# Sliding-window attention and a sentence-level MoE on one core: a fixed-order pipeline in place of a scheduled one

## Chip, cores, metric

The kernel runs on one core of one Trainium2 chip. The metric is the device time of one execution, in microseconds. Each run is marked fast or slow by its state. A ratio compares the fast runs alone of a kernel with fast runs of the kernel before, taken in the same rounds and on the same chip; the interval beside it is the 95% interval. A time in us is the median of all runs, slow ones included, so a ratio is not quite the ratio of two medians; where a slow run moves a median, the text says so. By these ratios a kernel counts as faster or slower if the difference is clear of 2%.

TensorE does the matrix products (matmuls) and writes them to PSUM, its accumulator memory; VectorE and ScalarE do the elementwise work, GpSimd some of the rest; the DMA engines move data between main memory (HBM) and SBUF, the working memory of the engines. MoE stands for mixture of experts, here the dense layers after attention.

## The reference

```python
B, H, S, D = 8, 8, 576, 64                       # attention
scores = q @ k.T / sqrt(D), allowed where |i - j| <= 32
attn   = softmax(scores);  a = attn @ v
x = a, heads side by side                        # (8, 576, 512)

pooled = x.mean(axis=1)                          # MoE: one expert per batch
logits = pooled @ w_gate                         # 8 experts
e      = argmax(logits);  g = softmax(logits)[e]
out    = g * (relu(x @ w1[e]) @ w2[e])           # 512 -> 1024 -> 512
```

The expert of a batch is known only when its whole attention is done. Its weights are 4.2 MB in fp32.

## The kernel before

A scheduler orders the instructions; the source says only what depends on what. The parts that matter here:

```python
def attention(b):
    # q, k, v: five loads each, 128 positions x 8 heads x 64: rows of 256 bytes
    ...
    nc.vector.tensor_copy(dst[:, 0:4, :, :], srt[:, 0:4, :, :])        # cast to bf16
    ...
    for hp in range(4):                                                # q and k: 40 transposes
        tp = ps1.tile([P, S], BF16, name="tp", tag="psA")
        for t in range(NST):
            nc.tensor.transpose(tp[:, SO[t] : SO[t] + ST[t]],
                src[0 : ST[t], t, 2 * hp : 2 * hp + 2, :], id_bf[0 : ST[t], 0 : ST[t]])
        nc.vector.tensor_copy(dst[:, hp, :], tp)                       # step 1 on both sides
    ...
    nc.tensor.matmul(sp[h][:, 0:mw], id_bf, ma, start=True, stop=False)   # -400 mask, by matmul
    nc.tensor.matmul(sp[h][0:J, off : off + RL[kb]], kTs[...], qTs[...], start=False, ...)
    nc.scalar.activation(et[h][:, eo : eo + mw], sp[h][:, 0:mw], Exp, scale=0.125)
    ...
    for t in range(NST):                                               # attention times V
        contribs = [(t, SO[t] - RLO[t], stl, 0)]                       # own keys: 128 columns
        if t >= 1:       contribs.append((t - 1, SO[t] - RLO[t - 1], 32, 0))
        if t + 1 < NST:  contribs.append((t + 1, 0, 32, stl - 32))
        for ci, (kb, lo, m, pr) in enumerate(contribs):                # shape outside,
            for h in range(H):                                         # heads inside
                nc.tensor.matmul(avp[pr : pr + m, base : base + 65],
                    Es[h][0:J, EOFF[kb] + lo : EOFF[kb] + lo + m], vaug[0:J, kb, h, :],
                    start=(ci == 0 and (h % 4) == 0), stop=False, tile_position=(0, pr))
        # reciprocal of the row sums and product on VectorE, four transposes, copy on ScalarE
    ...
def moe(xTt, lgi, gwb, b):
    nc.sync.dma_start(w1s32, moe_w1[ds(ereg, 1)][0]...)                # fp32
    nc.vector.tensor_copy(w1s, w1s32)                                  # cast on VectorE
    ...
for b in range(B):
    xTt = attention(b)
    if prev is not None: moe(*prev)
    lgi, gwb = gate(xTt)
    prev = (xTt, lgi, gwb, b)
```

The softmax here doesn't subtract the row's maximum and nothing guards it: scores larger than these inputs give would overflow.

## Time and profile before

| | before |
|---|---|
| median of its four runs in the first comparison | 386.8 us (383.93 to 389.44; the fourth took 1344.75 and is an outlier) |
| one middle batch | 42.3 us |
| TensorE busy, share of the span | 80% |
| mean granted TensorE clock | 0.852 |
| 16 DMA engines busy on loads and stores | 70.6% |

A group's row in the profile has line, engine, operation, output <- inputs, shapes and count; then busy time and the mean duration of one in ns; then the idle time ahead of it and what ended that. Matmul durations overlap, so what one matmul costs is read from a run of them. The chain of waits has start, length and what ran; `x16` is sixteen instructions merged. From the groups of the kernel before, attention times V:

```profile
L221 PE MATMUL avp<-vaug,etile 128*32 128x65 f16 (+3 forms) x832 | 44.9, 212 | 0.0
```

### The profile page before, as it was taken

The numbers are of one execution on the slowest core, as the hardware profiler recorded it, in microseconds if no ns is written. First come the engines' busy times: TensorE is split into PE (matmuls) and PEld (weight loads), VectorE is DVE, ScalarE is ACT, GpSimd is POOL, SyncE is SP. The second block draws the span as 40 slices with busy tenths as digits, with TensorE's granted clock in tenths as the row PEclk, the third lists the DMA queues.
The fourth block names the chain that finished last, engine by engine and source line by source line (L and its number), as shares of the span: only waits on it lengthen the run. The fifth ranks groups of instructions, "written<-read, shape, count | busy, mean of one in ns | idle before, by whom it ended". The sixth has DMA issues, their size and how long they took to land.

```text
span 384.9 us, 6511 instructions
## 1 busy us (share of the span) xinstructions
PE 307.4 (80%) x2656; PEld 176.6 (46%) x2656; DVE 165.9 (43%) x349; ACT 153.8 (40%) x353; POOL 7.9 (2%) x31
## 2 busy tenths in 40 slices
PE   0397498699958997699969997799859995893395
PEld 0234244474445554475345554565337444551262
DVE  0634562651467153652476055633385046501310
ACT  1044126163622536153723455253716362352052
POOL 1400000000000000000000000000000000000000
PEclk9998558589995999599986997599978999598599
DMA  9999049905889189936897289927996495015803
GB/s 160 210 208 162 3 157 346 202 7 160 278 273 212 51 219 381 222 67 179 305 285 161 83 236 371 195 48 211 345 258 119 149 292 218 0 54 181 325 0 124
DMA packets 130861, 71.74 MB, mean 186 GB/s; under 512 B 113936, under 2 KB 113936, under 8 KB 130832
## 3 DMA queue, kind: packets, MB, share of 16 engines
q1 hardware_dynamic: 130832, 71.33, 70.6%
q8 instruction: 21, 0.34, 0.4%
q14 instruction: 8, 0.07, 0.1%
HBM read 61.88 MB, written 9.44 MB: 185 GB/s over the span
## 4 chain that ended last, share of the span: by engine, by line
PE 70%; DVE 17%; DMA 6%; issue 4%; POOL 1%; SPq 0%; ACT 0%; DVEq 0%; POOLq 0%; ACTq 0%
PE op L340 18%; PE hpa L322 11%; PE hpb L326 10%; PE tp L162 8%; PE spAB L185 7%; PE avp L221 6%; PE spAB L194 6%; DVE xs L235 5%; DMA w2s<-in_moe_w_dram 4%; DVE w1s L312 4%; DVE w2s L314 4%; PE xtp L245 4%; DMA w1s<-in_moe_w_dram 2%; DVE linv L232 2%; DVE kbf L148 1%
## 5 line engine op out<-in xcount | busy, mean ns | idle before, releaser
L322 PE MATMUL hpa<-xTt,w1s 128*128 128x288 f16 x256 | 77.3, 331 | 12.2 <-DVE w1s L312 12.2
L326 PE MATMUL hpb<-xTt,w1s 128*128 128x288 f16 x256 | 76.6, 328 | 0.0
L203 ACT ACTIVATE etile<-spAB 128x480 f16<-128x480 f32 (+1 forms) x128 | 54.7, 550 | 48.3 <-PE spAB L194 47.4
L340 PE MATMUL op<-w2s,hT 128*128 128x512 f16 (+1 forms) x320 | 71.3, 380 | 0.0
L245 PE MATMUL xtp<-id_f,xs 128*128 128x128 f16 (+1 forms) x160 | 25.1, 254 | 41.0 <-DVE xs L235 40.2
L250 ACT COPY xTt<-xtp 128x512 f16<-128x512 f16 (+1 forms) x40 | 21.7, 542 | 83.2 <-PE xtp L245 83.2
L340 PEld LDWEIGHTS <-hT 128*128 128x128 f16 (+1 forms) x320 | 31.4, 100 | 37.2 <-issue 3.4
L347 ACT ACTIVATE osb<-op,gwb 128x512 f32<-128x512 f32 (+1 forms) x40 | 27.4, 686 | 43.7 <-PE op L340 43.7
L221 PE MATMUL avp<-vaug,etile 128*32 128x65 f16 (+3 forms) x832 | 44.9, 212 | 0.0
L330 ACT ACTIVATE hT<-hpa 128x288 f16<-128x288 f32 x64 | 26.2, 410 | 42.7 <-PE hpa L322 42.7
L221 PEld LDWEIGHTS <-etile 128*32 128x32 f16 (+3 forms) x832 | 37.1, 110 | 5.8 <-issue 1.6
L322 PEld LDWEIGHTS <-w1s 128*128 128x128 f16 x256 | 28.6, 112 | 23.0 <-DVE w1s L312 12.3
L266 DVE COPY lg<-lgp 1x8 f32<-1x8 f32 x8 | 1.2, 154 | 86.3 <-PE lgp L261 86.2
L232 DVE RECIPROCAL linv<-avp 128x8 f32<-128x8 f32 (+1 forms) x40 | 8.1, 203 | 67.1 <-PE avp L221 67.1
L245 PEld LDWEIGHTS <-xs 128*128 128x128 f16 (+1 forms) x160 | 9.8, 104 | 55.8 <-DVE xs L235 52.6
L326 PEld LDWEIGHTS <-w1s 128*128 128x128 f16 x256 | 28.5, 111 | 10.5
L235 DVE TENSOR_TENSOR xs<-avp,linv 128x256 f16<-128x256 f32 (+1 forms) x80 | 30.1, 417 | 1.4
L194 PE MATMUL spAB<-qTs,kTs 64*128 64x192 bf16 (+2 forms) x320 | 29.0, 249 | 0.0
L162 PE MATMUL tp<-id_bf,qbf 128*128 128x128 bf16 (+1 forms) x160 | 17.3, 236 | 14.3 <-DVE qbf L148 12.8
L333 ACT ACTIVATE hT<-hpb 128x288 f16<-128x288 f32 x64 | 25.9, 405 | 0.0
L255 DVE TENSOR_REDUCE pooledT<-xTt 128x4 f32<-128x2304 f16 x8 | 20.4, 2553 | 11.3 <-ACT xTt L250 11.3
L194 PEld LDWEIGHTS <-kTs 64*128 64x128 bf16 (+1 forms) x320 | 11.4, 97 | 29.8 <-issue 27.0
(51 smaller groups left out, 220.3 us busy)
## 6 DMA issues: line engine op xcount, KB each, us to landing
w1s<-in_moe_w_dram SPq DMA_DIRECT2D x8, 2048.0 KB, 8.1
w2s<-in_moe_w_dram SPq DMA_DIRECT2D x8, 2048.0 KB, 13.3
raw_q<-in_q_dram SPq DMA_DIRECT2D x32, 256.0 KB, 7.3
raw_k<-in_k_dram SPq DMA_DIRECT2D x32, 256.0 KB, 5.2
raw_v<-in_v_dram SPq DMA_DIRECT2D x32, 256.0 KB, 3.6
out_dram<-osb SPq DMA_DIRECT2D x32, 256.0 KB, 2.2
raw_q<-in_q_dram SPq DMA_DIRECT2D x8, 128.0 KB, 5.1
raw_k<-in_k_dram SPq DMA_DIRECT2D x8, 128.0 KB, 4.9
```

Of the source, the lines that this page charges most:

```text
L162: nc.tensor.transpose(tp[:, SO[t] : SO[t] + ST[t]], src[0 : ST[t], t, 2 * hp : 2 * hp + 2, :], id_bf[0 : ST[t], 0 : ST[t]],)
L185: nc.tensor.matmul(sp[h][:, 0:mw], id_bf, ma, start=True, stop=False, skip_group_check=True,)
L194: nc.tensor.matmul(sp[h][0:J, off : off + RL[kb]], kTs[hoff : hoff + D, hp, KO[kb] : KO[kb] + J], qTs[hoff : hoff + D, hp, RLO[kb] : RHI[kb]],
L203: nc.scalar.activation(et[h][:, eo : eo + mw], sp[h][:, 0:mw], mybir.ActivationFunctionType.Exp, bias=0.0, scale=0.125,)
L221: nc.tensor.matmul(avp[pr : pr + m, base : base + 65], Es[h][0:J, EOFF[kb] + lo : EOFF[kb] + lo + m], vaug[0:J, kb, h, :], start=(ci == 0 ...
L235: nc.vector.tensor_tensor(xs[0:stl, bk * 256 : (bk + 1) * 256].rearrange("p (h4 d) -> p h4 d", h4=4), hv[:, bk, :, 0:64], linv[0:stl, bk, ...
L245: nc.tensor.transpose(xtp[:, dt, 0:stl], xs[0:stl, dt * P : (dt + 1) * P], id_f16[0:stl, 0:stl],)
L322: nc.tensor.matmul(hpa, lhs, xTt[:, dt, 0:N1A], start=(dt == 0), stop=(dt == NDT - 1),)
L326: nc.tensor.matmul(hpb, lhs, xTt[:, dt, N1A:S], start=(dt == 0), stop=(dt == NDT - 1),)
L330: nc.scalar.activation(hT[:, ft, 0:N1A], hpa, mybir.ActivationFunctionType.Relu)
L340: nc.tensor.matmul(op[0:stl, :], hT[:, ft, SO[t] : SO[t] + stl], w2s[:, ft, :], start=(ft == 0), stop=(ft == NFT - 1),)
L347: nc.scalar.activation(osb[0:stl, :], op[0:stl, :], mybir.ActivationFunctionType.Copy, bias=0.0, scale=gwb[0:stl],)
```

## The change

The intent: take the order out of the scheduler's hands, hide attention's VectorE and ScalarE work under the dense MoE matmuls of the batch two before, load q and k in rows of 2304 bytes, cast weights in the DMA, and replace the mask matmuls by one product after the exponential. Positions come in interleaved (nine to a row of the load), so q and k are transposed in 64-row pieces and un-interleaved by a strided copy. Attention works on two heads per tile, with even and odd heads cut differently because V is loaded flat. The MoE runs in pieces of four matmuls between the pieces of attention. The core of the diff, shortened:

```diff
+    ctx.enter_context(tc.manual_schedule())
...
+            for name, dst in (("q", qT), ("k", kT)):
+                xb = castp.tile([P, J, 2, D], BF16, name=f"{name}bf", tag="qkbf", bufs=4)
+                nc.vector.tensor_copy(xb, r.rearrange("p h j d -> p j h d"))
+                for j in range(J):
+                    for pp in range(2):
+                        nc.tensor.transpose(tps[pp][:, j, :], xb[lo : lo + G, j, :, :], ...)
+                for pp in range(2):
+                    nc.vector.tensor_copy(t, tps[pp].rearrange("p j g -> p g j"))
+                yield
...
-                    nc.tensor.matmul(
-                        sp[h][:, 0:mw], id_bf, ma,
+            nc.vector.tensor_tensor(et, et, mask, ALU.mult)
...
+        nc.gpsimd.tensor_copy(vaug[:, :, 0:D], vraw)
...
-            for ci, (kb, lo, m, pr) in enumerate(contribs):
-                for h in range(H):
+            for h in (0, 2, 4, 6, 1, 3, 5, 7):
+                ...   # two parts per head: 128 columns, then 64 columns
+                for t, off, m, pr in parts:
                     nc.tensor.matmul(
...
-        nc.vector.tensor_copy(w1s, w1s32)
+        nc.gpsimd.dma_start(w1s, moe_w1[ds(ereg, 1)][0]...)     # fp32 -> fp16 in the DMA
...
+                # last MoE tile (64 rows): two column halves, tile_position=(0, 64 * c)
...
+    for n in range(B + LEAD):                                   # LEAD = 2
+        gens = [moe(n - LEAD), attention(n)]                    # one piece of each in turn
+        run_all(gens)
```

## The prediction

> **What bounds the kernel now.** I read the page first, then the chain of waits by time, then a table of stretches of one middle batch, then the timeline of that batch engine by engine.
>
> ```profile
> span 384.9 us, 6511 instructions
> ...
> PE 307.4 (80%) x2656; PEld 176.6 (46%) x2656; DVE 165.9 (43%) x349; ACT 153.8 (40%) x353; POOL 7.9 (2%) x31
> ...
> PEclk9998558589995999599986997599978999598599
> ...
> PE 70%; DVE 17%; DMA 6%; issue 4%; POOL 1%; SPq 0%; ACT 0%; DVEq 0%; POOLq 0%; ACTq 0%
> ...
> L167 DVE COPY qTs<-tp 128x576 bf16<-128x576 bf16 x32 | 14.2, 443 | 2.1 <-PE tp L162 1.0
> ```
>
> The chain that ended last is TensorE for 70% and VectorE for 17%; no other engine is near full. The clock row has a dip in each of the later batches: part of TensorE's "busy" is half-speed work.
>
> One batch (180.42 to 223.3 us), by stages; the columns are stretch, length, then each engine's busy time, granted clock, DMA share, GB/s:
>
> ```profile
> 180.42:184.30 3.88, 3.88 (x43) 2.59 (x42) 3.65 (x17) 0.89 (x3) 0.26 (x1) 1.00 0.87 203
> 184.30:190.50 6.20, 6.20 (x57) 2.16 (x56) 1.97 (x4) 5.56 (x14) 0.00 (x0) 1.00 0.86 321
> 190.50:202.20 11.70, 6.97 (x122) 4.99 (x120) 8.12 (x15) 3.55 (x7) 0.00 (x0) 0.87 1.08 294
> 202.20:214.30 12.10, 11.44 (x69) 7.78 (x70) 6.54 (x10) 5.44 (x16) 0.00 (x0) 0.71 0.61 128
> 214.30:223.30 9.00, 9.00 (x49) 4.02 (x48) 0.00 (x0) 3.54 (x7) 0.00 (x0) 1.00 0.43 133
> 223.30:265.60 42.30, 37.56 (x334) 22.05 (x334) 20.29 (x43) 19.00 (x45) 0.26 (x1) 0.84 0.77 212
> ```
>
> The stages are the q/k transposes (3.9 us), mask matmuls, scores and exponentials (6.2), attention times V with its transposes (11.7), the first MoE matmul (12.1) and the second (9.0). The last row is the whole next batch: 42.3 us. So 385 is about 8 x 42, plus a start of some 15 us and an end in which the last batch's MoE waits for its weights. In the third stage VectorE is on the path, as the chain shows for the same batch:
>
> ```profile
> 192.78 0.78 PE avp L221 x24
> 193.56 0.02 issue
> 193.58 0.22 DVE linv L232
> 193.83 0.76 DVE xs L235 x2
> 194.58 2.20 DVE w1s L312
> 196.78 0.12 DVE linv L232
> ```
>
> Each 0.78 us of matmuls is followed by a VectorE normalisation, and a weight cast of 2.2 us gets in front of the next one. TensorE idles, its clock falls to half at about 199 us, and the first MoE matmul runs its first 6 us at half speed (0.24 us for one 288-column matmul, later 0.12).
>
> **What the Trainium skill says.** (1) "Vector Engine (DVE) Microarchitecture Reference", section "Performance modes": packed 2-byte operands run two elements a cycle only with an innermost step of 1. The trace agrees for the present PSUM copy: 443 ns for 576 elements is 576/2/0.96 = 300 ns plus 143 fixed. The new copies read PSUM with a step of 64; no run shows that; my estimate from the page is 600 + 143 = 743 ns. (2) "VectorE: DVE Perf Modes", "The perf-mode tier table": a 16-bit tensor product in SBUF reaches 2x; its fp32 formula's 151 fixed cycles give an estimate of (1568/2 + 151)/0.96 = 974 ns for the new mask product. The kernel before has no such instruction. (3) "TensorE: Matmul & The Clock Gate", "Part 4: PE-mode transpose": transposes do not count as activity for the clock gate. The trace agrees: at 48.6 us, 40 transposes run for 5.65 us at a granted clock of 0.50, and it only rises at about 59 us, some 5 us after real matmuls begin. (4) "DMA: Bandwidth & Descriptors", "SWDGE vs HWDGE vs iDMA": a DMA that casts must be issued from GpSimd. No DMA of this trace casts.
>
> **The change part by part.**
> - *Weight DMA that casts.* Removes 16 VectorE casts of 2.28 us (36.6 us, 4.6 a batch, the worst of them in the third stage), and with two batches of lead the weights are asked for some 40 us before use. It also removes the weight wait of the last batch: 7.8 us of DMA, 2.3 of cast and about 2 of cold clock.
> - *0/1 mask product.* Removes 16 mask matmuls a batch (20.3 + 16.6 us busy in all; in the chain 0.41 and 0.51 us for each two, 3.7 us a batch). Adds 4 VectorE products of 0.97 = 3.9 us a batch, between the last exponential and the work that needs it.
> - *Long q/k reads.* In this trace stretches with weights only move 380 to 410 GB/s, with q/k/v only (256-byte rows) about 200. After: weights 33.5 MB / 0.39 = 86 us, q and k 18.9 / 0.39 = 48, flat V still in 256-byte rows 9.4 / 0.2 = 47, output 9.4 / 0.3 = 31: 212 us against some 260. Not the bound in either kernel, as long as the loads are early, and they are.
> - *The price of long reads.* The layout interleaves positions (nine to a row), so 72 transposes of 64 rows a batch take the place of 40, and the 8 copies out of PSUM become strided: 0.74 instead of 0.44 us. The q/k casts are 4 of 1152 elements, 1152/2/0.96 + 167 (from 1234 ns for 2048) = 0.77 us. V's cast moves to the idle GpSimd.
> - *Second MoE matmul.* The last 64 rows are done as two column halves side by side: saves up to 0.9 us a batch.
> - *Fixed order.* VectorE's order is now cast q, two copies, cast k, two copies, while TensorE has only one MoE piece between two attention pieces. I walk this chain, since each engine waits in order.
>
> One middle phase, what ends last at each step:
> (a) gate tail on VectorE and ScalarE: 1.55 us (349.7 to 351.26 in the trace).
> (b) one half of the heads: cast q 0.77; 18 transposes 0.8 (estimate: the 65-column matmuls take 0.93 us for 24, 39 ns each, a little more here) and 0.05 of signalling; copies 1.49; cast k 0.77, which stands behind them in VectorE's order; transposes 0.85; copies 1.49; first scores 0.3; then ScalarE: 3136 columns of exponentials at the measured 0.97 columns/ns (427 ns for a mean of 416) = 3.2, and four relus at 0.31 = 1.2, with 0.1 tail; mask product 0.97; signals 0.2: 12.2 us. Two halves: 24.4. Against this TensorE has 4 x 0.8 transposes, 40 score matmuls at 70 ns = 2.8, and twelve MoE pieces of 4 x 0.121 = 5.8: under 12 us of work. It waits half of the time.
> (c) attention times V, on TensorE: 5 x 0.75 + 1.15 of transposes + 3 x 0.48 + 6 half-tiles of the second MoE matmul at 4 x 0.219 = 5.25: 11.6 us. VectorE's 1.25 us a tile is hidden here.
> (d) gate: copy 0.6, pooling reduce 2.55, small matmuls and signals 0.4: 3.6.
> Sum 1.55 + 24.4 + 11.6 + 3.6 = 41.2 us, against 42.3. What was saved on TensorE is given back as waiting.
>
> Whole run: start 10; phases 0 and 1 are attention alone, 2 x (24.4 - 2.4 + 7 at VectorE's pace + 3.6 + 1.55 = 34 to 36) = 70; six phases of 41.2 = 247; phases 8 and 9 are MoE alone, 16 x 0.484 + 8 x 0.875 + 0.95 = 15.7 each, 31; last output 3. Sum 361. For the clock I add 0.5 us a phase (below): 364.
>
> **The rivals.**
> *Cold clock.* In (b) only the MoE pieces count as activity, 0.48 us in each 3.2 of the transposes. The trace dropped to half speed after stalls of this kind, and needed 5 to 6 us of dense matmuls to recover. Then a pair of heads in the scores costs TensorE about 3.0 us instead of 1.75, more than ScalarE's 2.2: +1.4 a half, transposes +0.5 a half, and the start of (c) +2: up to 6 us a phase, so 47 and about 397 in all. For it: the dips in the clock row. Against it: in (c) attention is mixed with the densest MoE work, so the worst dip of before goes. Some of both is likely; I counted only a little because the next rival pulls the other way.
> *Everything hides.* If casts and copies run ahead of TensorE, it is the bound: 3.2 + 2.8 + 3.75 + 1.15 + 0.3 + 7.75 + 7.95 = 27 us a phase, and 10 + 70 + 162 + 31 + 3 = 276. For it: that is plainly the intent, and a fixed order with piece counts of 24 and 25 looks tuned by someone. Against it: VectorE's order above, where cast k cannot pass the copies of q. Half-way would be 320.
> *VectorE worse than thought.* If the odd outer count of nine denies the q/k casts the fast mode, each takes 1.37, +2.4 a phase, +17 in all.
> *DMA.* Casting at a lower rate, or GpSimd's descriptors late: 40 us of lead hides it.
>
> **Range and chances.** 364 from the walk; its error is some 3 us a phase either way, which over six to eight phases is 20 to 25; the cold clock stretches it upward to about 400, hiding downward to about 330. Range 330 to 402. Against 389: faster by over 2% (below 381.6) 0.68, within 2% 0.16, slower (above 397) 0.16.
>
> **What would show it.** Right: a phase of 40 to 43 us; TensorE waiting for q/k casts and for the mask product, VectorE on the chain for 40% or more; strided copies near 743 ns; product near 974; last MoE phases near 16 us with no weight wait. Cold clock: a mean grant under 0.75 with halves in the scores. Wrong: phases of 30 us or less with TensorE busy throughout (then casts ran ahead), or weights and V among the longest waits.

## The result

| | before | changed |
|---|---|---|
| median | 386.8 us | 487.55 us |
| ratio (95% interval) | | 1.2646 (1.2531 to 1.2762) |
| one middle phase | 42.3 us | 55 to 58 us |
| DMA busy | 70.6% of 385 us | 46% of 487 us |
| mean granted clock | 0.852 | 0.816 |

The changed kernel is a quarter slower; 364 was predicted, in a range of 330 to 402. Its page and two of its groups:

```profile
span 487.3 us, 6487 instructions
...
PE 358.5 (74%) x2656; PEld 196.6 (40%) x2656; DVE 199.8 (41%) x371; ACT 156.5 (32%) x353; POOL 42.6 (9%) x68
...
PEclk9999999999766865797665966698675776688999
...
L270 PE MATMUL avp<-vaug,etile 128*128 128x65 f16 (+4 forms) x640 | 105.0, 230 | 6.6 <-DVE etile L228 6.6
...
L188 DVE COPY qT<-tp 128x576 bf16<-128x576 bf16 x32 | 22.8, 753 | 12.6 <-PE tp L181 12.6
```

Attention times V has fewer matmuls than before (640, not 832) and takes 105.0 us instead of 44.9. One matmul's duration is nearly the same (230 and 212 ns); what is gone is the overlap. The strided copy takes 753 ns, as predicted (743).

The same middle phase by stages (transposes and first half's scores to the second half's; its last scores; attention times V; then the whole phase, with the gate), with the columns of the prediction's table:

```profile
221.60:246.00 24.40, 17.33 (x159) 8.41 (x155) 13.99 (x23) 8.97 (x23) 4.25 (x5) 0.66 0.91 217
246.00:250.50 4.50, 4.50 (x30) 1.80 (x28) 0.98 (x1) 3.48 (x10) 0.00 (x0) 0.56 0.88 171
250.50:276.40 25.90, 25.18 (x144) 14.30 (x142) 7.02 (x21) 7.07 (x14) 0.00 (x0) 0.74 0.06 21
...
221.60:279.20 57.60, 47.33 (x335) 24.66 (x331) 24.54 (x46) 19.53 (x44) 4.25 (x5) 0.70 0.49 119
```

In the third row TensorE is busy for 25.18 of 25.9 us: this is no waiting. The chain of waits of the changed kernel, first in the transposes, then in attention times V:

```profile
226.22 1.41 DVE qT L188 x2
227.63 1.27 DVE kbf L174
...
228.94 0.48 PE tp L181 x18
229.43 1.42 DVE kT L188 x2
...
255.15 2.79 PE avp L270 x16
257.94 1.07 PE hp L369 x4
...
267.12 2.16 PE avp L270 x16
269.28 0.97 PE op L381 x4
```

The upper part is VectorE's order, as the prediction's walk has it: k's cast (1.27 us) stands behind the copies of q. The lower part is new: sixteen matmuls of 65 columns take 2.79 us while the clock is at half (the four MoE matmuls of 288 columns behind them take 1.07) and still 2.16 us when it is full (four of 512 columns take 0.97), that is 174 and 135 ns each. In the kernel before, 24 of them took 0.93 us at full clock, start to end of the last (194.76 us).

### The profile page after: what moved, and what is told of

Same layout as the page of the kernel before. It is cut to its first block, busy times and chain, and to the rows that moved or that the text cites. A ratio compares the mean times of both kernels' runs of the same rounds, so it can differ in the third digit from the quotient of the medians.

```text
span 487.3 us, 6487 instructions
## 1 busy us (share of the span) xinstructions
PE 358.5 (74%) x2656; PEld 196.6 (40%) x2656; DVE 199.8 (41%) x371; ACT 156.5 (32%) x353; POOL 42.6 (9%) x68
## 4 chain that ended last, share of the span: by engine, by line
PE 62%; DVE 25%; ACT 7%; issue 3%; POOL 2%; ACTq 0%; POOLq 0%
PE avp L270 19%; PE hp L369 16%; PE op L381 12%; PE sp L214 5%; ACT etile L223 5%; DVE kT L188 5%; DVE qT L188 5%; DVE pooledT L317 4%; PE tp L181 4%; DVE kbf L174 4%; DVE etile L228 3%; DVE qbf L174 3%; PE op L394 2%; PE xtp L296 2%; ACT osb L387 1%
## 5 line engine op out<-in xcount | busy, mean ns | idle before, releaser
L369 PE MATMUL hp<-xTt,w1s 128*128 128x288 f16 x512 | 116.6, 379 | 0.2 <-ACT osb L387 0.2
L270 PE MATMUL avp<-vaug,etile 128*128 128x65 f16 (+4 forms) x640 | 105.0, 230 | 6.6 <-DVE etile L228 6.6
L373 ACT ACTIVATE hT<-hp 128x288 f16<-128x288 f32 x128 | 52.7, 411 | 122.1 <-PE hp L369 118.5
L270 PEld LDWEIGHTS <-etile 128*128 128x128 f16 (+4 forms) x640 | 68.1, 107 | 49.9 <-issue 8.8
L223 ACT ACTIVATE etile<-sp 128x352 f16<-128x352 f32 (+2 forms) x128 | 55.5, 504 | 63.9 <-PE sp L214 63.7
L381 PE MATMUL op<-w2s,hT 128*128 128x512 f16 x256 | 69.8, 408 | 0.0
L228 DVE TENSOR_TENSOR etile<-etile,mask 128x1568 f16<-128x1568 f16 x32 | 31.2, 976 | 75.2 <-ACT etile L223 75.2
L214 PE MATMUL sp<-qT,kT 64*128 64x192 bf16 (+2 forms) x320 | 41.6, 323 | 9.2 <-DVE kT L188 8.6
L214 PEld LDWEIGHTS <-kT 64*128 64x128 bf16 (+1 forms) x320 | 15.4, 111 | 44.9 <-issue 26.6
L381 PEld LDWEIGHTS <-hT 128*128 128x128 f16 x256 | 23.1, 103 | 22.2 <-issue 3.2
L188 DVE COPY qT<-tp 128x576 bf16<-128x576 bf16 x32 | 22.8, 753 | 12.6 <-PE tp L181 12.6
## 6 DMA issues: line engine op xcount, KB each, us to landing
wg_sb<-in_moe_w_gate_dram SPq DMA_DIRECT2D x1, 16.0 KB, 11.6
```

Source lines behind the costliest of these rows:

```text
L188: nc.vector.tensor_copy(t, tps[pp].rearrange("p j g -> p g j"))
L214: nc.tensor.matmul(sp[bank][r0 : r0 + rows, off : off + w], kk[lo : lo + D, k0 : k0 + rows], qq[lo : lo + D, q0 : q0 + w], start=True, sto ...
L223: nc.scalar.activation(et[:, e0 : e0 + w], sp[par][:, 0:w], ACTF.Exp, bias=0.0, scale=0.125,)
L228: nc.vector.tensor_tensor(et, et, mask, ALU.mult)
L270: nc.tensor.matmul(pv[par][pr : pr + m, col : col + 65], et[r0 : r0 + rows, e0 : e0 + m], vaug[r0 : r0 + rows, vslot(h, t), :], start=st, ...
L369: nc.tensor.matmul(hp, w1s[:, dt, ft * P : (ft + 1) * P], xTt[:, dt, c0:c1], start=(dt == 0), stop=(dt == NDT - 1),)
```

## Theories

*Theory S (array shape).* Neighbouring matmuls of a head now alternate between 128 and 64 output columns, so the array changes its tiling at every instruction, and each change costs a drain. The Trainium skill says so on the page "TensorEngine Tiling (Array Packing)", section "Key Properties": changing the tiling mode, not just the tile, drains TensorE. It gives no size. The prediction did not use this sentence.
*Rival C (clock).* The matmuls are slow because TensorE runs at half clock.
*Rival A (same columns).* The second part of a head adds to the PSUM columns that the first part has just written; that dependence, not the shape, breaks the overlap.
Beside these, the prediction's own doubts were to be tested: the slow q/k casts, VectorE's order, the cold clock.

## Experiments

All outputs are right. The median of the kernel before was 384.4 to 386.8 us. The diffs are shortened, some to an outline.

### 1. Group attention times V by shape

```diff
-            for h in (0, 2, 4, 6, 1, 3, 5, 7):
-                for t, off, m, pr in parts:
+            for p in (0, 1):                       # all first parts, then all second parts
+                for h in (0, 2, 4, 6, 1, 3, 5, 7):
+                    t, off, m, pr = todo[h][p]
```

> The changed kernel with attention times V issued in groups: first the first part of all eight heads, then the second part of all, so that neighbours have the same array shape. Theory S (each change of array shape between neighbouring matmuls, or two in a row into the same PSUM columns, costs a drain): the 16 matmuls of a tile fall from 2.0 to 2.8 us to 0.65 to 1.0 us; with 640 matmuls at about 0.155 us less 0.04 that is 70 us, so about 415 us. Rival C (the half-speed clock is what makes these matmuls slow): they stay above 1.8 us for 16 and the time stays within 2% of 487.

Measured: 405.26 us (one of its four runs is slow; the fast ones took 403.94, 404.17 and 406.34), ratio to before 1.0503 (1.0377 to 1.0628): 82 us less than the changed kernel. It was run at another time. The chain of waits in attention times V:

```profile
258.10 0.60 PE hp L374 x4
258.70 0.50 PE avp L275 x16
...
261.01 0.97 PE op L386 x4
```

Sixteen take 0.50 us, 31 ns each. S's number is met and a little more. C as the only cause is out: at full clock the fourth tile takes 0.73 us of the chain here and 2.16 us in the changed kernel. The mean granted clock rose from 0.816 to 0.879, so part of the 82 us is the clock. I split it so: in the phase at 221.6 us attention times V itself takes 11.35 us of the chain, here 0.81 + 0.50 + 0.50 + 0.73 and about 0.7, so 8 us less a phase, 64 in eight. The rest I put down to MoE pieces in the same stretch that now run at the full clock; no run isolates it.

### 2. Alternate the shapes, but not on the same columns

```diff
+            order = [(hl[0], 0)]
+            for a in range(7):
+                order += [(hl[a + 1], 0), (hl[a], 1)]     # next head's first part between
+            order += [(hl[7], 1)]
```

> The changed kernel with attention times V issued so that the shape still changes at every matmul, but two in a row never write the same PSUM columns (first part of the next head before the second part of this one). If the change of shape costs: still 2.0 to 2.8 us for 16, time about 487. If what costs is that a matmul adds to columns that the one before has just written: like e1, about 415 us.

Measured: 460.85 us, ratio 1.1932 (1.1816 to 1.2048). The last tile of attention times V on the timelines of three runs, first the changed kernel, then this run, then the grouped kernel (start, length with the last one's drain, engine, line). The granted clock is 1.00 in all three:

```profile
213.57 2.06 PE L270 MATMUL avp<-vaug,etile 128*32 128x65 f16 x16
```

```profile
206.28 1.62 PE L279 MATMUL avp<-vaug,etile 128*32 128x65 f16 x16
```

```profile
221.33 0.76 PE L275 MATMUL avp<-vaug,etile 128*32 128x65 f16 x16
```

Counted from the loops, the array shape changes 14, 10 and 2 times within these sixteen matmuls: this order is not quite "at every matmul", since neighbours at its ends and where even heads give way to odd ones have one shape. The length follows the count: (2.06 - 0.76) / 12 and (1.62 - 0.76) / 8 are both 0.11 us a change. The fourth tile says the same: 2.32, 2.09 and 0.89 us (at 209.27, 202.20 and 218.45 us, clock 1.00) with 15, 13 and 2 changes, again 0.11 us a change. So the number of changes accounts for the times, whether or not neighbours write the same columns, and these tiles leave nothing for rival A. The 12 changes a batch that this order saves (two in each of four tiles, four in the last) are worth an estimated 10 us in eight batches; the run is 27 us faster. The granted clock is better too (0.875); how much of the rest it explains is not settled.

That it is the shape and not the place in the array is suggested by the q/k transposes: neighbours alternate between the upper and the lower 64 rows at one shape, and 18 of them take 0.48 us of the chain (228.94 us of the changed kernel), 27 ns each.

### 3. The kernel before, head by head

```diff
-            for ci, (kb, lo, m, pr) in enumerate(contribs):
-                for h in range(H):
+            for h in range(H):
+                for ci, (kb, lo, m, pr) in enumerate(contribs):
```

> The kernel before, with attention times V head by head (the two or three parts of one head after each other), as the changed kernel has it; nothing else. Theory S: 832 matmuls at 0.14 us in place of 0.04, up to 80 us more, about 460 us. Rival C: within 2% of 387.

Measured: 456.09 us, ratio 1.1831 (1.1726 to 1.1937), 71 us more than before by swapping two loops. The first row is the first tile of a batch on the timeline of the kernel before, the second the same tile in this run; the granted clock is 1.00 in both:

```profile
190.48 0.93 PE L221 MATMUL avp<-vaug,etile 128*128 128x65 f16 x16
```

```profile
229.16 2.23 PE L221 MATMUL avp<-vaug,etile 128*128 128x65 f16 x16
```

Within these sixteen the shape changes once in the kernel before and 15 times here: (2.23 - 0.93) / 14 = 93 ns a change. The mechanism is the same in both kernels and of about the same size. Over the five tiles of a batch this order has 83 changes in place of 6, an estimated 57 of the 71 us; most of this run's later tiles moreover ran at half clock.

### 4. Fast q/k casts by padding the destination

The q/k casts measured 1.34 us, not the 0.77 of the walk. By the Trainium skill's rule for the two-port mode ("Vector Engine (DVE) Microarchitecture Reference", "Performance modes"), the outermost counts of source and destination must both be even, or equal. Both views have nine rows; if the contiguous destination is taken as one run of 1152, they are not equal.

```diff
-                xb = castp.tile([P, J, 2, D], BF16, ...)
-                nc.vector.tensor_copy(xb, r.rearrange("p h j d -> p j h d"))
+                xb = castp.tile([P, J, 2 * D + 16], BF16, ...)       # rows can't be merged
+                nc.vector.tensor_copy(xb[:, :, 0 : 2 * D]..., r.rearrange("p h j d -> p j h d"))
```

> The changed kernel with the q/k casts written to rows padded by 16 elements, so that source and destination both have nine outer rows. If the slow cast comes from the odd outer count not matched by the destination: 1.34 us falls to 0.77 us for each of 64 casts; of four per batch three to four are on the chain, so 14 to 18 us less, about 471 us. If the cast is slow for the two-level source pattern as such: still 1.34 us, time unchanged.

Measured: 485.03 us, ratio 1.2557 (1.2441 to 1.2673): no gain worth the name, although the cast does become fast. The timeline of VectorE and GpSimd says why:

```profile
168.00 2.13 POOL L235 CAST vaug<-raw_v 128x2304 f16<-128x2304 f32 x1
168.87 2.13 DVE L174 CAST kbf<-raw_k 128x1152 bf16<-128x1152 f32 x1
...
180.08 0.82 DVE L174 CAST qbf<-raw_q 128x1152 bf16<-128x1152 f32 x1
```

The cast at 180 us takes 0.82 us. The one at 168.87 takes 2.13: V's cast runs on GpSimd until 170.13, and 170.13 + 0.82 is 170.95, to within 0.05 us the end of k's cast. The skill's page "SBUF — State Buffer", section "SBUF: two separate sides", states that a two-port VectorE instruction and a GpSimd instruction exclude each other for their whole length; this trace agrees. The slow casts of the changed kernel are not in that mode and ran beside GpSimd at 1.34 us.

### 5. The same, with V's cast on ScalarE

```diff
-        nc.gpsimd.tensor_copy(vaug[:, :, 0:D], vraw)
+        nc.scalar.copy(vaug[:, :, 0:D], vraw)      # emitted at the end of the batch before
```

> The changed kernel with the padded, fast q/k casts (as e4) and, beyond e4, V's cast moved from GpSimd to ScalarE; attention times V as in the change. If e4 gained nothing because half of the fast k casts stood still until GpSimd's V cast had ended (2.1 us for one in the trace of e4): all casts at 0.8 us, 8 x 1.3 less than e4, and 2 at the start, about 473 us. If that wait was hidden: within 1% of 485.

Measured: 466.73 us, ratio 1.2148 (1.2067 to 1.2229), 18 us less than experiment 4 by the medians, where 12 were expected. It was run at another time. All casts are at 815 ns (there are 32 in the run; the expectation of experiment 4 says 64, a slip). The same two edits on the grouped kernel:

> Grouped attention times V (as e1) with the padded, fast q/k casts, and V's cast moved from GpSimd to ScalarE at the end of the attention of the batch before, so that no cast on GpSimd can run beside a fast cast on VectorE. If the last run's padded cast gained nothing because the k cast had to wait for GpSimd's V cast: all 64 casts at 0.8 us, about 2.1 us less per phase over eight phases: 405 less 14 to 19, about 389 us. If the casts are hidden anyway: within 1% of 405.

Measured: 395.08 us, ratio 1.0214 (1.0113 to 1.0316, unclear by the 2% rule), 10 us less than the grouped kernel where 14 to 19 were expected. So less of the casts lay on the chain than expected; which of them, I did not trace.

### 6. Both casts first

```diff
-            for name, dst in (("q", qT), ("k", kT)):
-                cast(name); transposes(name); copies(name); yield
+            for name in ("q", "k"): cast(name)
+            for name, dst in (("q", qT), ("k", kT)):
+                transposes(name); copies(name); yield
```

> Grouped attention times V with one change of VectorE's order: the casts of q and k both ahead of the transposes and copies of q, slow casts kept. If VectorE's order (cast q, copies q, cast k, copies k) is on the path as the prediction's walk has it: the k transposes can follow the q transposes at once, about 1.3 us less in each of two halves of eight phases, 405 less 15 to 20, about 387 us. If not: within 1% of 405.

Measured: 376.73 us, ratio 0.9772 (0.9672 to 0.9873, unclear by the 2% rule against the kernel before), 28 us less than the grouped kernel, more than expected. The chain of waits:

```profile
223.26 1.26 DVE qbf L175
224.53 1.26 DVE kbf L175
225.79 1.33 DVE qT L192 x2
227.12 1.34 DVE kT L192 x2
```

VectorE now works without a gap, and the transposes, which stood between its pieces, are no longer on the path. A phase takes 40.9 us instead of 44.5 (six phases from one gate to the sixth after it): two transpose runs of 0.5 to 0.7 us a half left the path, besides waits. My expectation counted k's cast, which only moved.

### 7. Useless work to keep the clock up

```diff
+                times = 3 if piece in (2, 3, 8, 9) else 1    # pieces beside the transposes
-                for dt in range(NDT):
+                for dt in list(range(NDT)) * times:
```

> Grouped attention times V with useless work added: the four MoE pieces that stand beside the q/k transposes are computed three times over (the last one counts), 32 more matmuls of 288 columns a phase, 3.9 us at full clock. If the half-speed clock in the scores costs what the rival of the prediction said (1.4 us a half and more after it), the added work, which lies in TensorE's waits, makes the kernel faster: 405 less 10 to 25, about 388 us. If the clock there costs nothing: the same or up to 20 us slower.

Measured: 401.34 us, ratio 1.0411 (1.0311 to 1.0511), against 1.0503 for the grouped kernel. It was run at another time. The intervals overlap, so by time this is inconclusive and less than expected. By the traces a phase takes 43.2 us instead of 44.5, with 3.9 us more TensorE work in it. The clock rows, first of the grouped kernel, then of this one:

```profile
PEclk9999999999959966799659966898669965999999
```

```profile
PEclk9999965555878989899899899899899898999999
```

In the middle phases the dips to 5 and 6 have gone. So the half-speed clock in the scores seems to cost a little time, some 1.3 us a phase in these two traces; that ScalarE's exponentials and VectorE's chain set the pace, so that no more comes back, is my reading.

### 8. One part alone: the casting weight DMA in the kernel before

```diff
-        ereg = nc.sync.value_load(...);  nc.sync.dma_start(w1s32, ...)
-        nc.vector.tensor_copy(w1s, w1s32)
+        ereg = nc.gpsimd.value_load(...);  nc.gpsimd.dma_start(w1s, ...)   # casts
```

> The kernel before with one part of the change alone: weights loaded by a casting DMA from GpSimd, no cast on VectorE. If the two casts of 2.2 us that the chain shows in each batch's attention stage, and the wait for the last weights, are what this part removes: about 4 us a batch and 3 at the end, 385 less 25 to 35, about 355 us. If the first MoE matmul's cold start stays as it is and the casts were only filling waits: 375 to 385.

Measured: 396.82 us, ratio 1.0277 (1.0168 to 1.0385, unclear by the 2% rule). One of its four runs is slow and was the profiled one; the fast runs took 394.41, 394.42 and 399.23 us, so the ratio holds and the trace is only a pointer. Both expectations are missed: the casts went and the kernel got no faster, by the interval even a little slower. Its chain of waits has loads that the kernel before did not wait for:

```profile
104.13 15.34 DMA raw_k<-in_k_dram
...
248.57 8.73 DMA raw_v<-in_v_dram
```

With 256-byte rows the q, k and V loads are slow (about 200 GB/s from 10 to 32 us of the kernel before), and here the weight transfers run beside them from another queue. That the two delay each other is my reading; no run isolates it. In the changed kernel, with long q/k rows, no load is among the long waits. The parts of the change are not independent.

### 9. All corrections together

Grouped shapes, fast casts with V on ScalarE, casts first, the small constant ahead of the masks, four output buffers; the last MoE tile plain.

> All together: grouped attention times V, fast casts with V's cast on ScalarE, casts first, the small constant ahead of the masks at the start, four output buffers in place of three, the last MoE tile as eight plain matmuls. By the sum of the parts: 405 less 17 (casts) less 15 (order) less 10 (start) less 5 (outputs), about 358 us, faster than the kernel before (385). If the parts hide one another: 370 to 390.

Measured: 362.21 us, ratio 0.9398 (0.9307 to 0.9488), nearer to the sum of the parts (358) than to the other branch. The start and the four output buffers were not run alone. That buffers ran short is visible in the grouped kernel: its chain waits 2.0 us for an output transfer in most middle phases (2.01 us at 222.19, 2.00 at 266.65); the combined kernel's chain has no such wait.

### 10. The pieces in another order

```diff
+    scores(0,0)A | gate of the batch before, q transposes of half 1 | scores(0,0)B
+    scores(0,1)A | k transposes of half 1 | scores(0,1)B | scores(1,0), scores(1,1)
+    av0 | av1, xt0 | av2, xt1 + q transposes of the next batch | av3, xt2 | av4, xt3 + k transposes ...
```

> The combined kernel with its pieces moved so that VectorE's q/k chain lies beside other work: the second half's transposes stand among the first half's scores, the next batch's first transposes among this batch's attention times V, and the gate's small matmuls wait until the next phase's first scores are out. If the 40.7 us of the combined kernel's phase are waits of the order: TensorE's own 27 us and ScalarE's 21 come nearer, 32 to 36 us a phase, 305 to 335 us in all. If ScalarE's exponentials or VectorE's 23 us of work set a floor beside the order: 38 to 40 us a phase, 345 to 358 us.

Measured: 299.48 us, ratio 0.7761 (0.7697 to 0.7826). This is better than either branch of the expectation. No work was added or removed; VectorE's chain now lies beside scores and attention times V, and the pooling's 2.55 us and the small matmuls behind it no longer stop TensorE. Adding back the column halves:

> The reordered kernel (c2) with the last MoE tile again as two column halves side by side, as the change has it. In the trace of the changed kernel 16 half-width matmuls took 1.01 us at full clock, the 8 plain ones 1.84 in the trace of the combined kernel: 0.8 us less in each of eight batches where TensorE is the bound, about 293 us. If the halves do not run side by side, or their four small output transfers cost as much: 298 to 302 us.

Measured: 295.27 us, ratio 0.7684 (0.7643 to 0.7726). The first fence is from the page of this run, the second is its stretch from 180 to 210 us, the third a step of its chain:

```profile
span 293.6 us, 6484 instructions
...
PEclk9999999999979997999899998999799979799998
```

```profile
180.00:210.00 30.00, 27.89 (x311) 16.50 (x311) 20.68 (x44) 19.41 (x44) 2.21 (x4) 0.94 0.91 237
```

```profile
159.61 0.99 PE op L439 x16
```

TensorE is busy for 27.9 of these 30 us and the clock stays near full. The sixteen half-width matmuls take 0.99 us; the eight plain ones took 1.84 in the reordered kernel before. In itself that part of the change does what it was meant to. By time 4 of the 6 us expected came; the two reordered kernels were run in different calls and their intervals overlap a little. In the two traces the middle phases hardly shorten: 30.7 us here, 30.3 to 31.6 in the reordered kernel before (from one last MoE tile to the next), with a granted clock of 0.94 here and 0.99 to 1.00 there from 150 to 210 us. In the two phases of MoE alone at the end the whole 0.85 us shows (15.85 us for 16.70). This version beats the kernel before by 23% and the changed kernel by 39% (295.27 against 487.55). It was run at another time.

## Why the prediction was wrong, point by point

- **The step that failed: "(c) attention times V, on TensorE: 5 x 0.75".** The 0.75 us a tile was carried over from the matmuls of before, 39 ns each. The rate belonged to their order as well as to their size. In the new order the five tiles took 1.63 + 2.79 + 2.78 + 2.16 + 1.99 = 11.35 us of the chain, not 3.75. Experiments 1 to 3 show the cause: the change of shape at every matmul, about 0.11 us each at full clock.
- **The rest of (c).** MoE pieces beside it ran partly at half clock: three pieces took 3.10 us for 1.44, six half-tiles 7.20 for 5.25; transposes 1.30 for 1.15. With the five tiles that is 22.95 us for 11.6. "In (c) attention is mixed with the densest MoE work, so the worst dip of before goes" was wrong while the shapes alternated, and right when they were grouped (the clock was 1.00 in the grouped kernel's stretch from 257.2 to 270 us).
- **(b) one half of the heads, 12.2 us.** Both halves, from the first transposes (225.60 us) to the rest of attention times V (252.45), took 26.85, against 24.4 with the first q cast in it. VectorE's order sets the path as walked. The casts are 1.34 us and not 0.77, as the rival "VectorE worse than thought" had it, for the reason it named (experiment 4). The scores ran at half clock, as the rival "cold clock" had it: granted 0.56 in 246 to 250.5 us.
- **(a) and (d), gate.** (d) took 4.0 us for 3.6. (a) was not VectorE's tail but TensorE's own work: 0.97 + 1.85 + 1.07 = 3.89 us, of which the walk had 1.55 and the q cast. The phase: 26.85 + 22.95 + 4.0 + 3.89 = 57.7; measured 57.6 for this one and 56.1 as the mean of six (336.6 us from 110.0 to 446.6); predicted 41.2.
- **Start and ends.** The start took 24.6 us for 10: the cast of a small constant on VectorE waits for GpSimd, which first builds all masks; it then lasts until about the end of V's cast on GpSimd (2.26 us for eight elements; 0.36 in the run with V's cast on ScalarE), and the q cast stands behind it. The two attention-only phases took 41.4 and 44 us for 35 each, the end 40.7 for 34.4. Sum: 24.6 + 85.4 + 336.6 + 40.7 = 487.3.
- **What held.** The strided copy (753 ns for 743), the mask product (976 for 974), no DMA bound (46% busy), and the walk itself. Without the changing shapes the kernel takes 44.5 us a phase and 405 us, 3 us a phase more than walked; the casts (four times 0.5 us over the walk) and the wait for an output transfer (2.0 us in most phases, not in the walk) are of that size. But 405 is still above the top of the range, so the sizes of cast and start were wrong too.
- **"Everything hides".** It was set aside because k's cast cannot pass q's copies. That is true of this order and no property of the work: reordered, with the column halves, the phase is 30.7 us (150.56 to 181.30), near the 27 of TensorE's own sum.

## What to carry to other kernels

When small matmuls overlap, their rate belongs to their neighbours: keep those of one array shape together, and do not carry a rate from one loop order into another. In a fixed order, write down each engine's queue and look for work that stands behind a copy or a reduce for no reason of data; moving it was worth more here (63 us, from 362 to 299) than all the corrected parts of the change together (23 us, from 385 to 362). When a faster instruction gains nothing, look at what else holds its ports.

## What the Trainium skill lacked or had wrong

- "TensorEngine Tiling (Array Packing)" says that a change of tiling mode drains TensorE, with no size. Here sixteen 65-column matmuls took 2.06 us with 14 changes and 0.76 us with two, both at full clock: about 0.11 us a change.
- "Vector Engine (DVE) Microarchitecture Reference", "Performance modes", lists as not measured whether encoded rows that touch are merged. Nine touching rows as destination ran slow (1.34 us), the same rows 16 elements apart fast (0.815 us). Whether the compiler or the engine merges them, no run here tells.
- "TensorE: Matmul & The Clock Gate" warns that recorded clock events have been observed to be unreliable, but not where. Here the first clock record of the changed kernel is at 123.6 us, and until then the profile reads 1.00, while runs of sixteen matmuls from 51 to 58 us took 2.77 and 2.78 us, as in later stretches at 0.50. So means over a whole run are probably too high: from 123.6 us on the changed kernel's is 0.75 (0.816 over all), the grouped kernel's from its first record at 107.3 us is 0.84 (0.879).
